# Seven weight blocks prepared on VectorE and kept in DRAM, instead of summed by DMA as they are loaded

## The chip, the cores and the metric

The kernel runs on one core of a Trainium2 chip. The metric is the device time of one execution in microseconds (us). Of the kernel before, three runs were timed: 599.13, 599.25 and 601.3 us, median 599.25. A further execution was profiled; all rows below come from it.

## The reference

Causal attention (2 sequences, 12 heads, 448 positions, 64 columns) is followed by two feed-forward layers on 896 tokens of 768 columns:

```
x = attention(q, k, v)                    # scaled scores, causal mask, softmax, times v
h = x @ w_in;  y = (h * clip(h + 3, 0, 6) / 6) @ w_out              # 768 -> 2048 -> 768
xn = y / sqrt(mean(y*y) + 1e-6) * rms_g
g = xn @ w_gate; val = xn @ w_val
out = (silu(g) * val) @ w_out2                                      # 768 -> 1536 -> 768
```

The weights reach the kernel as the bits of float64, so each block has to be narrowed to float32 on the chip.

## The kernel before

Tokens stand in two groups of 448 columns (g = 0, 1). Every product is taken in three matmuls of 128x128 by 128x448 (`mm3`): weights and data are both split into a high and a low half, and high*high, high*low and low*high are summed. Weights come in blocks of 128x768, numbered 0 to 108 in the order of their use; each holds six 128x128 tiles, so a block serves 18 matmuls, or 36 in `ff2_in`, where both groups use it.

The stages in order: attention, with `ff1_in(0)` beside its end; `ff1_in(1)`; `ff1_out(0)`; `ff1_out(1)` (blocks 48 to 63); `ff2_in` (gate and val, blocks 64 to 87); `strassen` (the last layer, blocks 88 to 108). `strassen` computes the last product by a fast scheme with seven block products of half the size in place of eight: seven products q in the order 1, 5, 6, 7, 3, 4, 2, each with three blocks n = 0 to 2, 378 matmuls in all. Its weight operands are quarters of `w_out2` and sums of them.

The way of a block: `w_load` brings it from DRAM, `w_split` narrows it if it is float64 (two passes on ScalarE, `w_join` on VectorE), `w_halves` writes `whi` on ScalarE, `w_low` writes `wlo` on VectorE and calls `w_load` for the block three later. There are three buffers for `c` (the float32 block) and four each for `whi` and `wlo`.

The operands of the last layer are prepared beside `ff2_in`: `b_prepare` loads one of the twelve float64 blocks into `braw` (a single buffer), `b_narrow` and `b_join` narrow its two sides, and `b_keep` stores them as half blocks of 128x384 into DRAM. Four quarters (named 1, 2, 12, 22) are so kept. Products 1, 3 and 2 load one of them. For products 5, 6, 7 and 4, `w_load` loads a first block and one step later `w_add` adds a second one onto it by a DMA with accumulation, issued from POOL; for 5 and 6 the sum is also stored, since 6 and 4 start from them.

The order on every engine is the order in which the code issues instructions: a clock of steps (nine products' matmuls in each, outside attention), and `at(delay, ...)` puts a piece of work some steps later. All loads and stores named here are issued from one queue, SP, in that order, and an instruction that waits holds up all that stand behind it on its engine.

Of the kernel before, what the change touches and what calls it, by code (L numbers as in the profile page):

```python
# [13 lines left out]
AF = mybir.ActivationFunctionType  # L14
ALU = mybir.AluOpType
# [6 lines left out]
NK = DM // 128  # L22
# [5 lines left out]
NP1 = 16  # L28
NN = NK // 2
ORDER = (1, 5, 6, 7, 3, 4, 2)  # L30
BLOCKS = {1: (1,), 2: (2,), 3: (22,), 5: (12, 1), 6: (5, 22), 7: (12, 22), 4: (2, 6)}
SIDES = {(0, 0): 1, (0, 1): 2, (1, 0): 12, (1, 1): 22}
NEGATED = (1, 22)
NSLOT = 79
MASK = -8e9
NRAW, NC_BUF, NW = 3, 3, 4

# [13 lines left out]
def fused_kernel(ctx: ExitStack, tc, qa, qb, ka, kb, v, w_in, w_out, w_gate, w_val, w_out2, rms_g, out):  # L51
# [5 lines left out]
    nc = tc.nc  # L57

    const = ctx.enter_context(tc.tile_pool(name="const", bufs=1))
    pool = ctx.enter_context(tc.tile_pool(name="pool", bufs=NSLOT))  # L60
    wpool = ctx.enter_context(tc.tile_pool(name="wpool", bufs=1))
# [3 lines left out]
    def psum(name):  # L65
        return pspool.tile([128, 512], F32, tag="ps", name=name)

    def slot(shape, name, dtype=F32):
        return pool.tile(shape, dtype, tag="a", name=name)

    def f32(ap):
        return ap.bitcast(F32)
# [15 lines left out]
    def at(delay, fn, *args):  # L88
        due[clock["now"] + delay].append((fn, args))
# [15 lines left out]
    srcs, kept, parts = [], {}, {}  # L105
# [12 lines left out]
    def w_load():  # L118
        n = state["load"]
        if n >= len(srcs):  # L120
            return
        state["load"] += 1
        if not isinstance(srcs[n], tuple):
            t = wpool.tile([128, 768, 2], U32, tag="raw", name=f"raw{n}", bufs=NRAW)
            nc.sync.dma_start(t.rearrange("p n t -> p (n t)"), srcs[n].bitcast(U32))
            raws[n] = t
            return
        if srcs[n][0] in ("in", "out"):
            found = [kept.pop(srcs[n])]
        else:  # L130
            q, k = srcs[n]
            for p in BLOCKS[q]:
                assert parts[p, k] == 768, (srcs[n], p)
            found = [kept[p, k] for p in BLOCKS[q]]
        c = wpool.tile([128, 768], F32, tag="c", name=f"c{n}", bufs=NC_BUF)
        nc.sync.dma_start(c, found[0])
        plain[n] = c
        if len(found) == 2:
            at(1, w_add, n, c, found[1])

    def w_add(n, c, src):
        nc.gpsimd.dma_start(c, src, accum_op=ALU.add)  # L142
        q, k = srcs[n]
        if q in (5, 6):
            at(2, b_keep, q, k, 0, c)

    def w_split():

# [13 lines left out]
    def narrowed(c, raw, beside):  # L162

        low, high = raw[:, :, 0], raw[:, :, 1]
        byte = raw.rearrange("p n t -> p (n t)").bitcast(U8).rearrange("p (n t) -> p n t", t=8)[:, :, 3]
        if c is not None:
            nc.scalar.activation(c, f32(high), AF.Prelu, scale=2.0 ** -112, alpha=2.0 ** 32)  # L167
        if beside:
            nc.gpsimd.tensor_scalar(low, byte, 1.0 / 32.0, -15.5 / 32.0, op0=ALU.mult, op1=ALU.add)
        else:  # L170
            nc.scalar.activation(low, byte, AF.Copy, scale=1.0 / 32.0, bias=-15.5 / 32.0)  # L171
        return low
# [23 lines left out]
    def w_low(n, c):  # L196
        hi, lo = splits[n]
        nc.vector.tensor_sub(lo, c, f32(hi))  # L198
        if n >= NRAW:
            w_load()  # L200
# [3 lines left out]
    def w_tile(n, j):  # L204

        if n not in used:
            used.add(n)
            splits.pop(n - 2, None)
            at(1, w_split)
        return tuple(t[:, j * 128:(j + 1) * 128] for t in splits[n])  # L210

    def mm3(ps, w, x, first, last, again=False):

        whi, wlo = w
        xhi, xlo = x
        nc.tensor.matmul(ps, whi, xhi, start=first, stop=False, skip_group_check=again)  # L216
        yield
        nc.tensor.matmul(ps, whi, xlo, start=False, stop=False, skip_group_check=again)  # L218
        yield
        nc.tensor.matmul(ps, wlo, xhi, start=False, stop=last, skip_group_check=again)  # L220
        yield
# [6 lines left out]
        at(3, b_narrow, column, part, raw)  # L228

    def b_narrow(column, part, raw):  # L230
        narrowed(None, raw, False)
        pairs = raw[:, :, 1].rearrange("p (k o c) -> p k o c", o=2, c=128)
        for odd in range(2):
            t = f32(pairs[:, :, odd])
            sign = -1.0 if SIDES[column % 2, odd] in NEGATED else 1.0
            nc.scalar.activation(t, t, AF.Prelu, scale=sign * 2.0 ** -112, alpha=2.0 ** 32)
        at(1, b_join, column, part, raw)

    def b_join(column, part, raw):
        pairs = raw.rearrange("p (k o c) t -> p k o c t", o=2, c=128)  # L240
        for odd in range(2):
            t = slot([128, 384], f"b{column}_{part}_{odd}")
            nc.vector.scalar_tensor_tensor(
                t.rearrange("p (k c) -> p k c", c=128).bitcast(U32), pairs[:, :, odd, :, 1], 3, pairs[:, :, odd, :, 0],
                ALU.logical_shift_left, ALU.bitwise_or)
            at(1, b_keep, SIDES[column % 2, odd], column // 2, 384 * part, t)

    def b_keep(p, n, o, t):
        if (p, n) not in kept:
# [155 lines left out]
    def ff1_in(g, w0):  # L405

        for m in range(NF1):
            ps = psum(f"h{g}_{m}")[:, :NT]
            for k in range(NK):
                yield from mm3(ps, w_tile(w0 + m, k), xs[g, k], k == 0, k == NK - 1)  # L410
            at(1, ff1_relu, g, m, ps)
        for k in range(NK):
            xs.pop((g, k))
# [20 lines left out]
    def ff1_out(g, w0):  # L434


        for m in range(NK):
            ps = psum(f"y{g}_{m}")[:, :NT]
            for k in range(NF1):
                i = m * NF1 + k  # L440
                yield from mm3(ps, w_tile(w0 + i // 6, i % 6), gs[g, k], k == 0, k == NF1 - 1)
            at(1, ff1_y, g, m, ps)
        for k in range(NF1):
            gs.pop((g, k))

    left, halves = {"split": set()}, {}
    SOURCE = {1: (0, 0), 2: (0, 1), 4: (1, 1), 7: (1, 0)}

    def sums_first(p):

        t = slot([128, NT], f"s1_{p}")
        nc.vector.tensor_add(t, left[1, 2 * p], left[1, 2 * p + 1])
        left["s1", p] = t
        nc.vector.tensor_sub(left[1, 2 * p], left[1, 2 * p], left[0, 2 * p])
        at(1, sums_second, p)

    def sums_second(p):
        if (1, p) not in left["split"]:
            at(1, sums_second, p)
            return  # L460
        a = left[0, 2 * p]
        nc.vector.tensor_sub(a, a, left["s1", p])
        left["s2", p] = a
        at(1, sums_third, p)

    def sums_third(p):
        t = slot([128, NT], f"s4_{p}")
        nc.vector.tensor_add(t, left[0, 2 * p + 1], left["s2", p])
        left["s4", p] = t

    def a_split(q, p):

        key = {5: ("s1", p), 6: ("s2", p), 3: ("s4", p)}.get(q)
        if key is None:
            g, odd = SOURCE[q]
            key = (g, 2 * p + odd)
        src = left[key]
        hi = slot([128, NT], f"ahi{q}_{p}", F32R)
        lo = slot([128, NT], f"alo{q}_{p}", F32R)
        if q in (1, 3):  # L480
            nc.scalar.mul(hi, src, -1.0)
        else:
            nc.scalar.copy(hi, src)
        halves[q, p] = (hi, lo)
        at(1, a_low, q, p, key, hi, lo, src)

    def a_low(q, p, key, hi, lo, src):
        if q in (1, 3):
            nc.vector.scalar_tensor_tensor(lo, src, -1.0, f32(hi), ALU.mult, ALU.subtract)
        else:  # L490
            nc.vector.tensor_sub(lo, src, f32(hi))
        left["split"].add((q, p))
        if q != 1:
            left.pop(key)
# [146 lines left out]
    def products():  # L641
        yield from ff1_in(0, 0)
        yield from ff1_in(1, NP1)
        yield from ff1_out(0, 2 * NP1)
        yield from ff1_out(1, 3 * NP1)
        for i in range(2 * NK):
            at(6 + 7 * i, b_prepare, i // 2, i % 2)
        yield from ff2_in(IN2)
        yield from strassen(OUT2)

    with tc.manual_schedule():
# [4 lines left out]
        def warm_up(n):  # L656
# [6 lines left out]
        nc.gpsimd.affine_select(  # L663
            out=mask[:, S - C:], in_=mask[:, S - C:], compare_op=ALU.is_ge, fill=MASK,
            base=0, pattern=[[-1, C]], channel_multiplier=1)
# [23 lines left out]
        for n in range(NRAW):  # L689
            plan[12 + 12 * n].append((1, w_load))  # L690
            plan[52 + 6 * n].append((1, w_load))
# [75 lines left out]
```

## Time and profile before

| | us |
|---|---|
| median of three timed runs | 599.25 |
| profiled execution, its own time | 599.7 |
| span of its instructions (first to last) | 597.9 |
| PE busy | 581.3 |
| VectorE (DVE) busy | 363.0 |
| ScalarE (ACT) busy | 357.1 |
| GpSimd (POOL) busy | 97.7 |

PE is the matmul side of TensorE. A matmul of 448 columns is shown as 0.36 to 0.37 us long, but the next one starts 0.20 us after it; so intervals between starts are to be read, not durations. PEclk is the granted clock of TensorE, where 1.00 is full speed.

### The profile page before, as it was taken

How to read it: one execution, taken by the hardware profiler on the slowest of the kernel's cores; microseconds unless marked ns; L12 is line 12 of the kernel's file. 1: busy time of each engine (PE TensorE's matmuls, PEld its weight loads, DVE VectorE, ACT ScalarE, POOL GpSimd, SP SyncE). 2: the span in 40 equal slices, each digit the busy share in tenths (PEclk: the TensorE clock that was granted, in tenths of full speed). 3: DMA queues.
4: the chain of work that ended last, by engine and by line, in shares of the span. 5: the costliest groups of instructions: out<-in, count | busy, mean ns of one | idle time of the engine just before them, and what ended most of it. 6: DMA issues, size and time to landing. Idle time of an engine off the chain costs nothing.

```text
span 597.9 us, 8936 instructions
## 1 busy us (share of the span) xinstructions
PE 581.3 (97%) x3138; PEld 508.4 (85%) x3138; DVE 363.0 (61%) x688; ACT 357.1 (60%) x694; POOL 97.7 (16%) x144
## 2 busy tenths in 40 slices
PE   8889999999999999999999999999999999995997
PEld 6557777778899999999999999999999999984996
DVE  4766767676455576563534576676767664725881
ACT  6998888787455688774325775646365442424450
POOL 4665454543000000010001000000000001111100
PEclk9999999999999999999999999999999999998999
DMA  8968776752233488864254655557565345597761
GB/s 230 275 196 253 230 242 215 213 185 84 77 105 112 184 308 310 322 217 158 85 188 150 212 189 187 200 193 267 177 213 185 133 144 121 158 203 193 204 184 62
DMA packets 41150, 113.06 MB, mean 189 GB/s; under 512 B 5649, under 2 KB 17873, under 8 KB 41105
## 3 DMA queue, kind: packets, MB, share of 16 engines
q1 hardware_dynamic: 38944, 107.42, 54.1%
q0 software_dynamic: 1728, 4.72, 4.8%
q8 instruction: 25, 0.41, 0.3%
q10 hardware_dynamic: 432, 0.34, 0.2%
q14 instruction: 21, 0.16, 0.1%
HBM read 90.05 MB, written 22.41 MB: 188 GB/s over the span
## 4 chain that ended last, share of the span: by engine, by line
PE 85%; ACT 6%; DMA 5%; issue 2%; DVE 1%; SPq 0%; POOLq 0%; ACTq 0%; DVEq 0%
PE f L216 10%; PE f L220 9%; PE f L218 9%; PE y L216 7%; PE y L218 7%; PE y L220 7%; PE h L220 7%; PE h L216 7%; PE h L218 7%; DMA c<-kept 5%; ACT sm L324 4%; PE o L384 3%; PE s L307 3%; PE t L358 3%; ACT pt L368 1%
## 5 line engine op out<-in xcount | busy, mean ns | idle before, releaser
L192 ACT CAST whi<-c 128x768 fp32r<-128x768 f32 x109 | 90.8, 834 | 117.6 <-DVE c L176 57.4
L198 DVE TENSOR_TENSOR wlo<-c,whi 128x768 fp32r<-128x768 f32 x109 | 108.3, 994 | 59.9 <-ACT whi L192 57.6
L216 PE MATMUL f<-yhi,whi 128*128 128x448 f32 x288 | 105.8, 367 | 0.0
L220 PE MATMUL f<-yhi,wlo 128*128 128x448 f32 x288 | 104.9, 364 | 0.0
L218 PE MATMUL f<-ylo,whi 128*128 128x448 f32 x288 | 104.0, 361 | 0.0
L220 PE MATMUL h<-xh,wlo 128*128 128x448 f32 x192 | 72.0, 375 | 0.0
L218 PE MATMUL h<-xl,whi 128*128 128x448 f32 x192 | 70.9, 369 | 0.0
L216 PE MATMUL y<-ghi,whi 128*128 128x448 f32 x192 | 70.5, 367 | 0.0
L216 PE MATMUL h<-xh,whi 128*128 128x448 f32 x192 | 70.4, 367 | 0.0
L220 PE MATMUL y<-ghi,wlo 128*128 128x448 f32 x192 | 70.0, 365 | 0.0
L218 PE MATMUL y<-glo,whi 128*128 128x448 f32 x192 | 69.3, 361 | 0.0
L176 DVE SCALAR_TENSOR_TENSOR c<-c,raw 128x768 uint32<-128x768 uint32 x56 | 55.8, 996 | 20.0 <-ACT raw L171 13.8
L342 POOL TENSOR_SCALAR sm<-sm,st 112x112 f32<-112x112 f32 (+1 forms) x96 | 56.0, 601 | 68.5 <-ACT pt L368 28.8
L220 PEld LDWEIGHTS f<-yhi,wlo 128*128 128x128 f32 x288 | 53.9, 187 | 5.4 <-issue 0.2
L218 PEld LDWEIGHTS f<-ylo,whi 128*128 128x128 f32 x288 | 54.1, 188 | 4.0
L216 PEld LDWEIGHTS f<-yhi,whi 128*128 128x128 f32 x288 | 54.1, 188 | 3.7 <-issue 0.2
L167 ACT ACTIVATE c<-raw 128x768 f32<-128x768 f32 x56 | 50.7, 906 | 3.9 <-DVE wlo L198 3.2
L324 ACT ACTIVATE sm<-sm,st 112x112 f32<-112x112 f32 (+3 forms) x96 | 49.6, 525 | 3.9 <-DVE st L317 3.8
L142 POOL DMA_DIRECT2D c<-kept x12 | 10.4, 865 | 222.0 <-DMA kept<-b 158.6
L220 PEld LDWEIGHTS h<-xh,wlo 128*128 128x128 f32 x192 | 36.0, 188 | 9.3 <-issue 6.7
L421 DVE SCALAR_TENSOR_TENSOR t<-t,h 128x448 f32<-128x448 f32 x32 | 19.8, 620 | 38.7 <-ACT t L417 38.7
L417 ACT ACTIVATE t<-h,half 128x448 f32<-128x448 f32 x32 | 20.5, 639 | 35.4 <-PE h L220 35.4
(109 smaller groups left out, 983.3 us busy)
## 6 DMA issues: line engine op xcount, KB each, us to landing
raw<-in_w_in SPq DMA_DIRECT2D x16, 768.0 KB, 5.3
raw<-in_w_out SPq DMA_DIRECT2D x16, 768.0 KB, 6.1
raw<-in_w_gate SPq DMA_DIRECT2D x12, 768.0 KB, 4.3
raw<-in_w_val SPq DMA_DIRECT2D x12, 768.0 KB, 4.3
braw<-in_w_out SPq DMA_DIRECT2D x12, 768.0 KB, 5.0
c<-kept SPq DMA_DIRECT2D x21, 384.0 KB, 3.7
keptin<-c SPq DMA_DIRECT2D x16, 384.0 KB, 2.7
c<-keptin SPq DMA_DIRECT2D x16, 384.0 KB, 3.0
```

Source lines behind the costliest of these rows:

```text
L167: nc.scalar.activation(c, f32(high), AF.Prelu, scale=2.0 ** -112, alpha=2.0 ** 32)
L176: nc.vector.scalar_tensor_tensor(bits, bits, 3, z, ALU.logical_shift_left, ALU.bitwise_or)
L192: nc.scalar.copy(hi, c)
L198: nc.vector.tensor_sub(lo, c, f32(hi))
L216: nc.tensor.matmul(ps, whi, xhi, start=first, stop=False, skip_group_check=again)
L218: nc.tensor.matmul(ps, whi, xlo, start=False, stop=False, skip_group_check=again)
L220: nc.tensor.matmul(ps, wlo, xhi, start=False, stop=last, skip_group_check=again)
L307: nc.tensor.matmul(ps[:C, o:o + n], tq[64 * j:64 * j + 64, i * C:(i + 1) * C], tk[64 * j:64 * j + 64, 0:n], start=True, stop=True)
L324: nc.scalar.activation(dst, dst, AF.Exp, scale=-1.0, bias=st[u][:, 0, c:c + 1], accum_out=st[u][:, 1, c:c + 1])
L342: nc.gpsimd.tensor_scalar(t[:, o:o + n], t[:, o:o + n], c, 1.0, op0=ALU.mult, op1=ALU.mult)
L417: nc.scalar.activation(t, ps, AF.Relu, bias=half, scale=1.0 / 6.0)
L421: nc.vector.scalar_tensor_tensor(t, t, 1.0, ps, ALU.min, ALU.mult)
```

## The change

All seven weight operands are made beforehand and kept in DRAM, so that the last layer loads one block for each of its 21. `w_add` and the stores of loaded sums are gone. The differences (5: first minus first, 7, 6, 4, named `bt`) are made on VectorE from the narrowed half blocks (`b_sums`, `b_rest`), and all stores go by half blocks. The twelve preparations begin with `ff1_out(1)`, one in six steps, in place of with `ff2_in`, one in seven. `b_narrow` has two full-width passes on ScalarE instead of one full and two half ones. Signs move from the weights to the data: a few subtractions change their order and two `-1` scalings fall away; the number of those instructions stays.

```diff
@@ -28,10 +28,8 @@
 NP1 = 16
 NN = NK // 2
 ORDER = (1, 5, 6, 7, 3, 4, 2)
-BLOCKS = {1: (1,), 2: (2,), 3: (22,), 5: (12, 1), 6: (5, 22), 7: (12, 22), 4: (2, 6)}
-SIDES = {(0, 0): 1, (0, 1): 2, (1, 0): 12, (1, 1): 22}
-NEGATED = (1, 22)
 NSLOT = 79
+PREP, BETWEEN = 4, 6
 MASK = -8e9
...
         if srcs[n][0] in ("in", "out"):
-            found = [kept.pop(srcs[n])]
+            src = kept.pop(srcs[n])
         else:
-            q, k = srcs[n]
-            for p in BLOCKS[q]:
-                assert parts[p, k] == 768, (srcs[n], p)
-            found = [kept[p, k] for p in BLOCKS[q]]
+            src = kept[srcs[n]]
+            assert parts[srcs[n]] == 768, srcs[n]
         c = wpool.tile([128, 768], F32, tag="c", name=f"c{n}", bufs=NC_BUF)
-        nc.sync.dma_start(c, found[0])
+        nc.sync.dma_start(c, src)
         plain[n] = c
-        if len(found) == 2:
-            at(1, w_add, n, c, found[1])
-
-    def w_add(n, c, src):
-        nc.gpsimd.dma_start(c, src, accum_op=ALU.add)
-        q, k = srcs[n]
-        if q in (5, 6):
-            at(2, b_keep, q, k, 0, c)
...
@@ -228,22 +215,41 @@
         at(3, b_narrow, column, part, raw)
 
     def b_narrow(column, part, raw):
-        narrowed(None, raw, False)
-        pairs = raw[:, :, 1].rearrange("p (k o c) -> p k o c", o=2, c=128)
-        for odd in range(2):
-            t = f32(pairs[:, :, odd])
-            sign = -1.0 if SIDES[column % 2, odd] in NEGATED else 1.0
-            nc.scalar.activation(t, t, AF.Prelu, scale=sign * 2.0 ** -112, alpha=2.0 ** 32)
+        c = f32(raw[:, :, 1])
+        narrowed(c, raw, False)
         at(1, b_join, column, part, raw)
+
+    got = {}
 
     def b_join(column, part, raw):
         pairs = raw.rearrange("p (k o c) t -> p k o c t", o=2, c=128)
+        n, j = divmod(column, 2)
         for odd in range(2):
             t = slot([128, 384], f"b{column}_{part}_{odd}")
             nc.vector.scalar_tensor_tensor(
                 t.rearrange("p (k c) -> p k c", c=128).bitcast(U32), pairs[:, :, odd, :, 1], 3, pairs[:, :, odd, :, 0],
                 ALU.logical_shift_left, ALU.bitwise_or)
-            at(1, b_keep, SIDES[column % 2, odd], column // 2, 384 * part, t)
+            got[odd, j] = t
+            if (odd, j) != (0, 1):
+                at(1, b_keep, {(0, 0): 1, (1, 0): 2, (1, 1): 3}[odd, j], n, 384 * part, t)
+        if j == 1:
+            at(1, b_sums, n, part)
+
+    def b_sums(n, part):
+        b_minus(5, n, part, got[0, 1], got[0, 0])
+        b_minus(7, n, part, got[1, 1], got[0, 1])
+        at(1, b_rest, n, part)
+
+    def b_rest(n, part):
+        b_minus(6, n, part, got[1, 1], got["t", 5])
+        b_minus(4, n, part, got[1, 0], got["t", 6])
+        got.clear()
+
+    def b_minus(p, n, part, a, b):
+        t = slot([128, 384], f"bt{p}_{n}_{part}")
+        nc.vector.tensor_sub(t, a, b)
+        got["t", p] = t
+        at(1, b_keep, p, n, 384 * part, t)
 
     def b_keep(p, n, o, t):
         if (p, n) not in kept:
...
-        nc.vector.tensor_sub(left[1, 2 * p], left[1, 2 * p], left[0, 2 * p])
+        nc.vector.tensor_sub(left[1, 2 * p], left[0, 2 * p], left[1, 2 * p])
         at(1, sums_second, p)
 
...
         a = left[0, 2 * p]
-        nc.vector.tensor_sub(a, a, left["s1", p])
+        nc.vector.tensor_sub(a, left["s1", p], a)
         left["s2", p] = a
         at(1, sums_third, p)
 
     def sums_third(p):
         t = slot([128, NT], f"s4_{p}")
-        nc.vector.tensor_add(t, left[0, 2 * p + 1], left["s2", p])
+        nc.vector.tensor_sub(t, left[0, 2 * p + 1], left["s2", p])
         left["s4", p] = t
 
     def a_split(q, p):
...
         lo = slot([128, NT], f"alo{q}_{p}", F32R)
-        if q in (1, 3):
-            nc.scalar.mul(hi, src, -1.0)
-        else:
-            nc.scalar.copy(hi, src)
+        nc.scalar.copy(hi, src)
         halves[q, p] = (hi, lo)
         at(1, a_low, q, p, key, hi, lo, src)
 
     def a_low(q, p, key, hi, lo, src):
-        if q in (1, 3):
-            nc.vector.scalar_tensor_tensor(lo, src, -1.0, f32(hi), ALU.mult, ALU.subtract)
-        else:
-            nc.vector.tensor_sub(lo, src, f32(hi))
+        nc.vector.tensor_sub(lo, src, f32(hi))
         left["split"].add((q, p))
         if q != 1:
             left.pop(key)
...
@@ -642,9 +642,10 @@
         yield from ff1_in(0, 0)
         yield from ff1_in(1, NP1)
         yield from ff1_out(0, 2 * NP1)
+        for i in range(2 * NK):
+            n, rest = divmod(i, 4)
+            at(PREP + BETWEEN * i, b_prepare, 2 * n + rest % 2, rest // 2)
         yield from ff1_out(1, 3 * NP1)
-        for i in range(2 * NK):
-            at(6 + 7 * i, b_prepare, i // 2, i % 2)
         yield from ff2_in(IN2)
         yield from strassen(OUT2)
 

```

PE's order is the same in both kernels. Three places where others differ:

SP and POOL in the last layer, before: `c91` to `c93` are the blocks of product 5, `c94` to `c96` of product 6, `c97` on of product 7; `kept12_0` is quarter 12 of block column 0. SP:

```order
L136 DMA c92_5103<-kept12_1_4503 128x768
L254 DMA kept5_1_5139<-c92_5103 128x768
L136 DMA c93_5156<-kept12_2_4945 128x768
L254 DMA kept5_2_5193<-c93_5156 128x768
L136 DMA c94_5220<-kept5_0_5083 128x768
L136 DMA c95_5260<-kept5_1_5139 128x768
L254 DMA kept6_0_5276<-c94_5220 128x768
L136 DMA c96_5297<-kept5_2_5193 128x768
L254 DMA kept6_1_5313<-c95_5260 128x768
L136 DMA c97_5338<-kept12_0_4062 128x768
L254 DMA kept6_2_5352<-c96_5297 128x768
```

Between the loads stand stores of sums, which wait for the accumulating loads. Those stand on POOL, in the same stage:

```order
L142 DMA c91_5044<-kept1_0_3839 128x768
L142 DMA c92_5103<-kept1_1_4281 128x768
L142 DMA c93_5156<-kept1_2_4721 128x768
L142 DMA c94_5220<-kept22_0_4064 128x768
L142 DMA c95_5260<-kept22_1_4505 128x768
L142 DMA c96_5297<-kept22_2_4947 128x768
L142 DMA c97_5338<-kept22_0_4064 128x768
L142 DMA c98_5374<-kept22_1_4505 128x768
L142 DMA c99_5405<-kept22_2_4947 128x768
```

Each adds a second quarter onto a block that SP has loaded. SP at the same place now:

```order
L132 DMA c91_5109<-kept5_0_3468 128x768
L132 DMA c92_5163<-kept5_1_3884 128x768
L132 DMA c93_5213<-kept5_2_4291 128x768
L132 DMA c94_5274<-kept6_0_3489 128x768
L132 DMA c95_5313<-kept6_1_3908 128x768
L132 DMA c96_5347<-kept6_2_4312 128x768
L132 DMA c97_5385<-kept7_0_3470 128x768
L132 DMA c98_5418<-kept7_1_3886 128x768
L132 DMA c99_5448<-kept7_2_4293 128x768
```

Nine loads stand one behind the other; the stores between them are gone, and POOL issues nothing any more in this stage.

VectorE in `ff1_out(1)` before, around blocks 54 to 58 (`ylo` belongs to the layer's result):

```order
L198 TENSOR_TENSOR wlo54_3337<-c54_3266,whi54_3336 128x768
L198 TENSOR_TENSOR wlo55_3361<-c55_3293,whi55_3360 128x768
L567 SCALAR_TENSOR_TENSOR ylo1_1_3392<-y1_1_3299,gvec_74,yhi1_1_3376 128x448
L198 TENSOR_TENSOR wlo56_3390<-c56_3323,whi56_3389 128x768
L198 TENSOR_TENSOR wlo57_3417<-c57_3349,whi57_3416 128x768
L198 TENSOR_TENSOR wlo58_3441<-c58_3374,whi58_3440 128x768
```

Here it has only the low halves of blocks and of the result. The same place now (`b` are narrowed half blocks, `bt` the differences):

```order
L229 SCALAR_TENSOR_TENSOR b0_0_0_3340<-braw0_0_3277 128x384
L229 SCALAR_TENSOR_TENSOR b0_0_1_3342<-braw0_0_3277 128x384
L185 TENSOR_TENSOR wlo54_3345<-c54_3266,whi54_3344 128x768
L185 TENSOR_TENSOR wlo55_3375<-c55_3295,whi55_3374 128x768
L567 SCALAR_TENSOR_TENSOR ylo1_1_3406<-y1_1_3301,gvec_74,yhi1_1_3390 128x448
L185 TENSOR_TENSOR wlo56_3404<-c56_3327,whi56_3403 128x768
L229 SCALAR_TENSOR_TENSOR b1_0_0_3432<-braw1_0_3372 128x384
L229 SCALAR_TENSOR_TENSOR b1_0_1_3434<-braw1_0_3372 128x384
L250 TENSOR_TENSOR bt5_0_0_3450<-b1_0_0_3432,b0_0_0_3340 128x384
L250 TENSOR_TENSOR bt7_0_0_3452<-b1_0_1_3434,b1_0_0_3432 128x384
L185 TENSOR_TENSOR wlo57_3437<-c57_3361,whi57_3436 128x768
L250 TENSOR_TENSOR bt6_0_0_3472<-b1_0_1_3434,bt5_0_0_3450 128x384
```

Four joins and four differences of 128x384 now stand between the `wlo` of blocks that PE is about to use.

SP in `ff1_out(1)` before, around blocks 56 to 60:

```order
L136 DMA c56_3323<-keptout_8_2913 128x768
L136 DMA c57_3349<-keptout_9_2943 128x768
L136 DMA c58_3374<-keptout_10_2973 128x768
L136 DMA c59_3405<-keptout_11_3011 128x768
L136 DMA c60_3429<-keptout_12_3041 128x768
```

It has loads of blocks alone. The same place now:

```order
L132 DMA c56_3327<-keptout_8_2913 128x768
L260 DMA kept1_0_3356<-b0_0_0_3340 128x384
L260 DMA kept2_0_3358<-b0_0_1_3342 128x384
L132 DMA c57_3361<-keptout_9_2943 128x768
L214 DMA braw1_0_3372<-in_w_out2 128x1536
L132 DMA c58_3388<-keptout_10_2973 128x768
L132 DMA c59_3421<-keptout_11_3011 128x768
L260 DMA kept3_0_3448<-b1_0_1_3434 128x384
L132 DMA c60_3455<-keptout_12_3041 128x768
L214 DMA braw0_1_3466<-in_w_out2 128x1536
L260 DMA kept5_0_3468<-bt5_0_0_3450 128x384
L260 DMA kept7_0_3470<-bt7_0_0_3452 128x384
```

Loads of `braw` and stores of half blocks, which wait for VectorE, now stand between the loads of blocks.

## Rows read from the trace of the kernel before

**Rows 1.** The page: span; busy time by engine.

```profile
span 597.9 us, 8936 instructions
PE 581.3 (97%) x3138; PEld 508.4 (85%) x3138; DVE 363.0 (61%) x688; ACT 357.1 (60%) x694; POOL 97.7 (16%) x144
...
```

**Rows 2.** Busy time by stretch; columns named in the first row.

```profile
core 0: us, PE busy (x) PEld busy (x) DVE busy (x) ACT busy (x) POOL busy (x), PEclk, DMA share, GB/s
215.80:274.10 58.30, 58.30 (x290) 54.05 (x289) 34.75 (x39) 40.81 (x55) 4.65 (x4) 1.00 0.80 282
274.10:333.00 58.90, 58.90 (x291) 54.29 (x290) 26.58 (x27) 25.84 (x36) 5.81 (x5) 1.00 0.43 142
333.00:508.46 175.46, 175.46 (x867) 162.34 (x867) 112.59 (x168) 96.68 (x140) 3.05 (x3) 1.00 0.55 184
508.46:537.62 29.16, 29.16 (x146) 26.84 (x144) 14.70 (x23) 10.41 (x19) 4.23 (x5) 1.00 0.73 181
537.62:554.70 17.08, 10.64 (x41) 8.57 (x41) 9.77 (x16) 9.15 (x16) 1.69 (x2) 0.80 0.74 187
```

**Rows 3.** Timeline of PE: first and last matmul of the last layer, three stops.

```profile
508.50 0.37 PE L216 MATMUL w<-ahi,whi 128*128 128x448 f32 x1
...
538.43 0.47 PE L216 MATMUL y<-ahi,whi 128*128 128x448 f32 x1 [0.64 <-ACT whi L192]
...
549.98 0.74 PE L216 MATMUL y<-ahi,whi 128*128 128x448 f32 x1 [4.63 <-ACT ahi L483]
551.57 0.74 PE L218 MATMUL y<-alo,whi 128*128 128x448 f32 x1 [0.85 <-DVE alo L491]
...
593.92 0.36 PE L220 MATMUL x<-ahi,wlo 128*128 128x448 f32 x1
```

**Rows 4.** Timeline of ACT behind the longest stop.

```profile
548.63 0.83 ACT L192 CAST whi<-c 128x768 fp32r<-128x768 f32 x1 [7.32 <-DMA c<-kept]
549.37 1.03 ACT L483 CAST ahi<-u 128x448 fp32r<-128x448 f32 x2
```

**Rows 5.** Part of the chain of waits: start us, us, what.

```profile
532.54 4.90 DMA c<-kept
537.46 0.32 SPq L254
...
537.88 4.25 DMA c<-kept
...
542.66 5.89 DMA c<-kept
```

**Rows 6.** What the SP queue waited for, 500 to 560 us.

```profile
SPq L254 <- DMA c<-kept: 30.7, 5, 8.0
```

**Rows 7.** DMA issues of the page: count, KB each, us to landing.

```profile
braw<-in_w_out SPq DMA_DIRECT2D x12, 768.0 KB, 5.0
c<-kept SPq DMA_DIRECT2D x21, 384.0 KB, 3.7
...
c<-kept POOLq DMA_DIRECT2D x12, 384.0 KB, 5.4
...
```

**Rows 8.** DMA issues, 215.8 to 274.1 us alone.

```profile
raw<-in_w_out SPq DMA_DIRECT2D x11, 768.0 KB, 6.4
...
```

**Rows 9.** Instructions by line and shape, 274.1 to 508.5 us.

```profile
L198 DVE TENSOR_TENSOR wlo<-c,whi 128x768 fp32r<-128x768 f32 x41 | 40.9, 999 | 20.3 <-ACT whi L192 20.1
L192 ACT CAST whi<-c 128x768 fp32r<-128x768 f32 x40 | 33.4, 834 | 54.0 <-DVE c L176 37.6 <-PE y L218 14.9 <-PE f L218 1.5
...
L167 ACT ACTIVATE c<-raw 128x768 f32<-128x768 f32 x24 | 21.4, 891 | 3.2 <-DVE wlo L198 3.2
...
L243 DVE SCALAR_TENSOR_TENSOR b<-braw 128x384 uint32<-128x384 uint32 x24 | 12.2, 551 | 0.0
...
L171 ACT ACTIVATE braw<-braw 128x768 uint32<-128x768 uint8 x12 | 10.7, 895 | 0.8 <-DMA braw<-in_w_out 0.8
```

**Rows 10.** Timeline of ACT in the second output layer.

```profile
289.35 0.84 ACT L192 CAST whi<-c 128x768 fp32r<-128x768 f32 x1 [2.80 <-PE y L218]
```

More of the change, by code (lines that the diff above doesn't have):

```diff
@@ L165, in narrowed @@
         byte = raw.rearrange("p n t -> p (n t)").bitcast(U8).rearrange("p (n t) -> p n t", t=8)[:, :, 3]
-        if c is not None:
-            nc.scalar.activation(c, f32(high), AF.Prelu, scale=2.0 ** -112, alpha=2.0 ** 32)
+        nc.scalar.activation(c, f32(high), AF.Prelu, scale=2.0 ** -112, alpha=2.0 ** 32)
         if beside:
```

## The prediction

> **What bounds the kernel now.** I read the page first: PE is busy for 581.3 of 597.9 us [rows 1]; so only time in which PE stops, or work that leaves PE, can move the end, and PE's list of matmuls stays as it is. Next the stretches [rows 2]: from 215.8 to 508.46 us PE is busy without a gap at full clock (before that lies attention, which the change doesn't touch); in 537.62 to 554.70 us it starts 41 matmuls in 17.08 us and its granted clock falls to 0.80. That is inside the last layer, the only place after 216 us where PE stands still. Then the timeline of PE there [rows 3]: a stop of 0.64 us that ends with a `whi`, one of 4.63 us that ends with an `ahi` on ACT, one of 0.85 us that ends with the `alo` behind it. The reader might blame the data halves `ahi`; ACT's own timeline says otherwise [rows 4]: the `ahi` that PE waited for is behind a `whi` for which ACT had been idle for 7.32 us, until a block from DRAM had landed. The chain of waits says why the block was late [rows 5]: accumulating load (4.90 us), SP's issue of the store of the sum, which waited for it, the next plain load (4.25), the next accumulating load (5.89). SP spent 30.7 us in this stage in front of such stores [rows 6], with the next blocks' loads queued behind. A block thus needs a plain load and an accumulating one in series, 3.7 and 5.4 us in the median [rows 7], and part of this does not overlap between blocks, while PE uses up a block in 18 matmuls.
>
> **What the stops cost.** From 333.00 to 508.46 us PE runs 866 matmuls (867 are shown, one reaches in from before) in 175.46 us [rows 2], one in 0.2026 us. The last layer has 7 x 3 x 6 x 3 = 378, which need 378 x 0.2026 = 76.6 us. It takes from 508.50 to 593.92 plus 0.20, 85.6 us [rows 3]. So 9.0 us are lost, the slow clock after the long stop included.
>
> **The change, part by part.**
>
> *Removed: twelve accumulating loads, six stores of loaded sums.* With one load per block, `w_low` of a block issues the load for the block three later, and PE takes 3 x 18 x 0.2026 = 10.9 us for three blocks. A plain load lands in 3.7 us [rows 7], then come `whi` (0.83) and `wlo` (1.0) [rows 9]: 5.5 of 10.9 us. `ff1_out(1)` runs just so, with the same sizes and the same 18 matmuls per block, and PE has no gap there in 58.90 us [rows 2]. I take the whole 9.0 us back. From both sides: it cannot be more, since PE would then run without a gap to the end; the least that this removal alone gives is nothing, if the blocks were late for another reason (a rival below). Nearest row: `ff1_out(1)`, hence the whole.
>
> *Added on VectorE: 24 differences of 128x384.* The trace has no subtraction of this size. A join of 128x384 takes 0.551 us and a two-operand pass over 128x768 0.999 [rows 9]; I take 0.55, the row with the same size, so 24 x 0.55 = 13.2 us (bounds: nothing and 24.0). None of it is on PE's path while VectorE has room: in `ff1_out(1)` it is busy for 26.6 of 58.9 us [rows 2], and five preparations (ten joins, eight differences) bring 18 x 0.55 = 9.9 us; in `ff2_in` 112.6 of 175.5 us are busy, and ten joins less and sixteen differences more make 3.3 us. Cost 0.
>
> *Moved: twelve preparations, from `ff2_in` into `ff1_out(1)` and the front of `ff2_in`.* Five of them (steps 4, 10, 16, 22 and 28 of the 32 of that layer) fall where a block lasts 3.65 us and not 7.3. What matters is how far ahead of PE the blocks are there. ACT's `whi` at 289.35 us began when PE left a block, after 2.80 us of idling [rows 10]: it is not short of data but of one of four buffers, so it writes for the block three later, 10.9 us ahead of its use. Of these `whi` and `wlo` take 1.8, and 9.1 are spare. A preparation puts two passes on ACT between them, 0.89 each [rows 9], 1.8 us, and on VectorE up to two joins and four differences, 3.3 us: 4.0 us stay. Cost 0. If the cover were gone, each would cost PE up to 5.1 us.
>
> *Queues.* SP carries 42 stores of half blocks in place of 24 and 6; those of `b` and `bt` now wait for VectorE with the loads of blocks 57 to 63 and of `raw` and `braw` behind them. Each stands in the order behind work that is due a step before it, and the load behind it waits for a `wlo` that VectorE does later still; so I count no hold. The bytes: `ff1_out(1)` has 142 GB/s, 8.4 MB in 58.9 us [rows 2]; five loads of 0.79 MB and 14 stores of 0.20 MB make 15.0 MB, 255 GB/s. The stretch before it ran at 282 GB/s with PE never stopped [rows 2]. Cost 0.
>
> *Load on the transfers.* At 282 GB/s a load of 768 KB landed in 6.4 us [rows 8], while `braw`, of the same size, takes 5.0 in its quieter stretch [rows 7]: 1.4 us more, which the 4.0 us that stay cover. The Trainium skill speaks against the change here (DMA: Bandwidth & Descriptors, Latency and other measured facts): HBM access takes 0.2 us on average and up to 2 at high load, so moving transfers into a stretch with others makes all of them slower; by that rule it would be 1.8 us for each (an estimate from the page), with the sum unchanged, and the slower rival below would set in 1.8 us earlier. The rows agree in direction.
>
> *Signs.* As many instructions as before, of the same shapes. Nothing.
>
> **The sum.** 599.7 (the profiled execution's own time) - 9.0 + 0 = 590.7 us. That execution is 0.45 us above the median of 599.25, so on the scale of the median 590.25; I put 590.4, leaving a little for a first block that comes late.
>
> **Rivals.**
>
> 1. *Part of the stop stays.* For it: all transfers of the last layer still share SP's queue with the stores of the result, and 0.73 to 0.74 of the DMA time was in use there [rows 2]. Against: the accumulating loads and the stores of sums go, and plain loads alone never held PE [rows 2, 10]. If half of the loss stays: 599.7 - 4.5 = 595.2.
> 2. *The data halves are the limit.* PE's longest stop ended with `ahi` [rows 3]; if ACT or VectorE were late with these on their own, single loads would not help. For it only that row; against it ACT's idle time of 7.32 us right in front [rows 4]. Time: 599.25 as before.
> 3. *Slower: ACT stands behind `braw` in `ff1_out(1)`.* ACT takes its work in order. If a `braw` (one buffer, loaded only after the join before it, behind SP's waiting stores) lands late, ACT stops and with it every `whi` behind. It decides from 4.0 us of lateness; to eat the whole gain, five preparations have to be 4.0 + 9.0 / 5 = 5.8 us late each, and for 0.5% above the old time (3.0 us more) 6.4. At 8 us: 5 x 4.0 = 20, so 599.7 - 9.0 + 20 = 610.7. For it: SP has waits of up to 8.0 us [rows 6]. Against: ACT waited for `braw` only 0.8 us in all twelve preparations [rows 9], which are as far behind their loads in steps (three) as now.
>
> **Chances and range.** Forecast 0.82, rival 1 0.11, rival 2 0.04, rival 3 0.03. The forecast alone: 589.3 (0.9 below, for runs that differ) to 591.8. The range takes in the near half of rival 1: 589.3 to 593.8. A measurement of this kernel tells about 0.5% from no change, 3.0 us: faster means under 596.25. Forecast and most of rival 1 are there, 0.92; within 0.5% are rival 2 and the rest of rival 1, 0.05; slower is rival 3, 0.03.
>
> **What the new profile would show.** If right: span about 588.9; the last layer takes 76.6 us with PEclk 1.00 throughout; no accumulating load, no wait of SP in front of a store for a load; ACT's `whi` there ends its idle time on PE, not on `c<-kept`; 24 differences near 0.55 us; PE without a gap from 274 us on. Wrong would be: an idle time of PE in `ff1_out(1)` or early `ff2_in` that ends with `whi` or `wlo` (rival 3, with ACT idle on `braw`), or one in the last layer that ends with `ahi` while ACT had the block in time (rival 2).

## The result, and the profile after

The changed kernel takes 590.41 us in the median of four runs (589.90 to 590.92); the kernel before, now with a fourth run beside it, 599.97. The ratio is 0.9839, with a 95% interval of 0.9814 to 0.9863. The profiled execution took 589.9 us over a span of 588.1. Of one kernel below (plain loads with six stores) one run in four took 1145 us, with no trace of it, and its median is given without it.

The page after: span, busy time by engine, PE's busy tenths and its granted clock in 40 slices.

```profile
span 588.1 us, 8933 instructions
PE 578.7 (98%) x3138; PEld 507.6 (86%) x3138; DVE 375.2 (64%) x712; ACT 356.5 (61%) x682; POOL 87.2 (15%) x132
...
PE   8899999999999999999999999999999999999997
...
PEclk9999999999999999999999999999999999999999
...
```

The stretch of before in which PE was busy for 10.64 of 17.08 us, at a clock of 0.80 [rows 2], is gone: neither PE's tenths nor its clock fall there. Of the busy times only VectorE's has grown, by 12.2 us [rows 1]; POOL has lost its 10.5 us of accumulating loads.

The stretches after, for `ff1_out(1)`, `ff2_in` and the last layer:

```profile
core 0: us, PE busy (x) PEld busy (x) DVE busy (x) ACT busy (x) POOL busy (x), PEclk, DMA share, GB/s
...
273.70:332.60 58.90, 58.90 (x291) 54.29 (x290) 34.41 (x43) 33.60 (x46) 5.82 (x5) 1.00 0.73 254
332.60:508.04 175.44, 175.44 (x867) 162.31 (x866) 116.18 (x174) 88.20 (x119) 1.17 (x1) 1.00 0.48 162
508.04:584.70 76.66, 76.65 (x380) 70.70 (x378) 49.43 (x77) 32.23 (x55) 0.00 (x0) 1.00 0.34 111
...
```

PE is busy throughout in all three, at full clock. `ff1_out(1)` now moves 254 GB/s in place of 142 and has VectorE busy for 34.4 us in place of 26.6 [rows 2]. The last layer takes up the window of 76.66 us.

First and last matmul of the last layer on PE's timeline:

```profile
508.08 0.37 PE L203 MATMUL w<-ahi,whi 128*128 128x448 f32 x1
...
584.32 0.37 PE L207 MATMUL x<-ahi,wlo 128*128 128x448 f32 x1
```

From start to start this is 76.24 us; before it was 593.92 - 508.50 = 85.42 [rows 3]. The difference, 9.18 us, is nearly the whole of the span's 9.8. Of the rest, 0.42 us lie in front of the last layer (508.50 to 508.08; the first matmul of `ff1_in` is already 0.43 us earlier, in a part that the change leaves alone), and 0.20 behind its last matmul.

ACT's timeline in the middle of the last layer; the bracket is its idle time and what ended it:

```profile
529.92 0.84 ACT L179 CAST whi<-c 128x768 fp32r<-128x768 f32 x1 [1.87 <-PE z L205]
530.66 1.03 ACT L486 CAST ahi<-u 128x448 fp32r<-128x448 f32 x2
...
```

Before, ACT waited here for a block from DRAM, up to 7.32 us [rows 4]. Now its `whi` waits until PE leaves a buffer, as in `ff1_out(1)` [rows 10]: the blocks are early.

The longest wait of the SP queue, 500 to 560 us:

```profile
SPq L132 <- DVE wlo L185: 47.5, 15, 7.1
...
```

No store of a sum stands in front of a load any more [rows 6]; SP waits for `wlo`, that is for a free buffer of `c`. Stores of the result still stand there, and SP waits 7.8 us in front of them, but PE has no gap.

The new and moved work by line and shape, 273.7 to 508 us (count, busy time and mean ns, idle time in front):

```profile
L229 DVE SCALAR_TENSOR_TENSOR b<-braw 128x384 uint32<-128x384 uint32 x24 | 12.3, 554 | 6.6 <-ACT braw L158 6.6
...
L154 ACT ACTIVATE braw<-braw 128x768 f32<-128x768 f32 x12 | 10.9, 906 | 10.1 <-DMA braw<-in_w_out 10.1
...
L250 DVE TENSOR_TENSOR bt<-b,bt 128x384 f32<-128x384 f32 x12 | 6.7, 555 | 0.3
L250 DVE TENSOR_TENSOR bt<-b,b 128x384 f32<-128x384 f32 x12 | 6.1, 552 | 0.0
```

A difference of 128x384 takes 552 to 555 ns. But ACT now waits 10.1 us in all for `braw`, before only 0.8 [rows 9]. Part of the reason stands in the DMA issues (count, KB each, median us to landing):

```profile
braw<-in_w_out SPq DMA_DIRECT2D x12, 768.0 KB, 5.7
...
c<-kept SPq DMA_DIRECT2D x21, 384.0 KB, 3.0
...
kept<-bt SPq DMA_DIRECT2D x24, 192.0 KB, 5.3
kept<-b SPq DMA_DIRECT2D x18, 192.0 KB, 2.5
```

A `braw` lands after 5.7 us in place of 5.0 [rows 7], a plain block of the last layer after 3.0 in place of 3.7. The longest of ACT's waits has a second reason: SP issues the load late. SP's timeline there, then ACT's:

```profile
355.10 0.79 SPq L260 DMA_DIRECT2D kept<-b  x2
355.98 0.45 SPq L214 DMA_DIRECT2D braw<-in_w_out  x1
...
```

```profile
362.57 0.91 ACT L154 ACTIVATE braw<-braw 128x768 f32<-128x768 f32 x1 [3.57 <-DMA braw<-in_w_out]
...
```

ACT was ready for this `braw` at 359.00, only 3.0 us after its load was issued; the code leaves three steps between them, 5.5 us of PE's time. Right in front of it SP stood until VectorE had written the `b` to be stored.

### The profile page after: what moved, and what is told of

Its sections match the earlier page's. It is cut to its first block, busy times and chain, and to the rows that moved or that the text cites. A ratio compares the mean times of both kernels' runs of the same rounds, so it can differ in the third digit from the quotient of the medians.

```text
span 588.1 us, 8933 instructions
## 1 busy us (share of the span) xinstructions
PE 578.7 (98%) x3138; PEld 507.6 (86%) x3138; DVE 375.2 (64%) x712; ACT 356.5 (61%) x682; POOL 87.2 (15%) x132
## 4 chain that ended last, share of the span: by engine, by line
PE 93%; ACT 6%; issue 1%; DVE 0%; DVEq 0%
PE f L203 10%; PE f L207 10%; PE f L205 10%; PE y L203 8%; PE y L207 8%; PE y L205 8%; PE h L207 7%; PE h L203 7%; PE h L205 7%; ACT sm L330 4%; PE o L390 3%; PE t L364 3%; PE s L313 3%; PE z L203 1%; PE z L207 1%; PE z L205 1%
## 5 line engine op out<-in xcount | busy, mean ns | idle before, releaser
L323 DVE CUSTOM_DVE_ANT_0 sm<-s,mask 112x112 f32<-112x112 f32 (+3 forms) x96 | 37.3, 443 | 5.9 <-PE s L313 5.6
```

The source lines that it names most:

```text
L323: nc.vector.tensor_tensor_reduce(dst, src, mask[:, S - n:], scale=-0.125, scalar=3e38, op0=ALU.add, op1=ALU.min, accum_out=st[u][:, 0, c:c ...
```

## Experiments

Each was timed beside the kernel before on the same chip (medians 599.2 to 600.5), and its ratio is to those runs; the first two rows are those of the result. The last layer is given from its first to its last matmul's start.

| kernel | median us | ratio to before (95%) | last layer us |
|---|---|---|---|
| before | 599.97 | | 85.42 |
| changed | 590.41 | 0.984 (0.981 to 0.986) | 76.24 |
| changed, late preparations | 590.54 | 0.986 (0.983 to 0.988) | 76.24 |
| before, early preparations | 599.02 | 1.000 (0.998 to 1.002) | 85.14 |
| before, no stores of sums | 591.50 | 0.988 (0.985 to 0.990) | 76.33 |
| changed, six stores added | 589.99 | 0.985 (0.981 to 0.988) | 76.24 |
| before, stores later | 594.99 | 0.992 (0.990 to 0.995) | 81.30 |
| before, stores later, fourth c | 590.72 | 0.985 (0.982 to 0.988) | 76.24 |
| before, fourth c | 592.69 | 0.988 (0.986 to 0.991) | 77.86 |
| changed, one preparation in 4 steps | 596.35 | 0.994 (0.991 to 0.997) | 76.24 |
| changed, differences 4 times | 614.94 | 1.024 (1.019 to 1.029) | 76.24 |
| changed, differences twice | 590.19 | 0.985 (0.981 to 0.989) | 76.24 |

**The two halves of the change apart.** The late preparations in the changed kernel:

```diff
-        for i in range(2 * NK):
-            n, rest = divmod(i, 4)
-            at(PREP + BETWEEN * i, b_prepare, 2 * n + rest % 2, rest // 2)
         yield from ff1_out(1, 3 * NP1)
+        for i in range(2 * NK):
+            n, rest = divmod(i, 4)
+            at(6 + 7 * i, b_prepare, 2 * n + rest % 2, rest // 2)
```

Expected: 

> The changed kernel, with the twelve preparations put back beside ff2_in (one in seven steps from its sixth step on). Theory A (the gain is the single plain load for each block of the last layer; when the blocks are prepared does not matter): PE again without a gap in the last layer, 76.2 us from its first to its last matmul, median within 0.3% of the changed kernel's 590.4 us. Rival C (the earlier preparation brought part of it, because the last layer's first loads wait for stores that come late): a stop of some us at the start of the last layer, 593 us or more.

First and last matmul of the last layer on PE's timeline:

```profile
508.58 0.37 PE L203 MATMUL w<-ahi,whi 128*128 128x448 f32 x1
...
584.82 0.37 PE L207 MATMUL x<-ahi,wlo 128*128 128x448 f32 x1
```

76.24 us, as in the changed kernel to 0.01 us. The other half, early preparations in the kernel before:

```diff
+        for i in range(2 * NK):
+            at(4 + 6 * i, b_prepare, i // 2, i % 2)
         yield from ff1_out(1, 3 * NP1)
-        for i in range(2 * NK):
-            at(6 + 7 * i, b_prepare, i // 2, i % 2)
```

Expected: 

> The kernel before, with its twelve preparations moved into ff1_out(1), one in six steps, and the sums still made by accumulating loads. Theory A: the stop stays, about 9 us lost in the last layer, median about 600 us. Rival C (the earlier preparation brought the gain): at most half of it is left, 595 us or less.

PE's timeline at the stops:

```profile
539.13 0.47 PE L216 MATMUL y<-ahi,whi 128*128 128x448 f32 x1 [1.64 <-ACT whi L192]
...
549.42 0.47 PE L216 MATMUL y<-ahi,whi 128*128 128x448 f32 x1 [1.80 <-ACT ahi L483]
551.01 0.74 PE L218 MATMUL y<-alo,whi 128*128 128x448 f32 x1 [1.12 <-DVE alo L491]
...
```

The stops are there again, the first longer and the second shorter than before [rows 3], 0.28 us less in all. So the whole gain comes from how the blocks are loaded, and none from when they are prepared. (The passes of `b_narrow` and the signs were not put back alone; a kernel below that has the old ones reaches 76.24 us too.)

**Accumulation or stores.** Six stores taken out of the kernel before:

```diff
-BLOCKS = {1: (1,), 2: (2,), 3: (22,), 5: (12, 1), 6: (5, 22), 7: (12, 22), 4: (2, 6)}
+BLOCKS = {1: (1,), 2: (2,), 3: (22,), 5: (12, 1), 6: (12, 22), 7: (12, 22), 4: (2, 22)}
...
         nc.gpsimd.dma_start(c, src, accum_op=ALU.add)
-        q, k = srcs[n]
-        if q in (5, 6):
-            at(2, b_keep, q, k, 0, c)
```

Expected: 

> The kernel before without the six stores of loaded sums; products 6 and 4 take quarters 12 + 22 and 2 + 22 in place of the stored sums, so their operands are other numbers; all twelve accumulating loads stay. Theory A in its narrow form (the stores in front of which SP waits for the accumulation put the blocks in series; without them plain load 3.7, accumulating load 5.4, whi and wlo 1.8 us take 10.9 of the 10.9 us that a block has): at most 1.5 us lost in the last layer, median 590 to 592.5 us. Rival B (the accumulating loads alone are too slow): at least 5 us still lost, 596 us or more.

Products 6 and 4 are here loaded from other quarters, as many and as large, so that no stored sum is needed; the kernel computes another result, and no load has to wait for a stored sum either. ACT's timeline in the middle of the last layer:

```profile
530.40 0.83 ACT L189 CAST whi<-c 128x768 fp32r<-128x768 f32 x1 [3.27 <-DMA c<-kept]
...
539.15 0.83 ACT L189 CAST whi<-c 128x768 fp32r<-128x768 f32 x1 [2.19 <-DMA c<-kept]
...
544.37 0.83 ACT L189 CAST whi<-c 128x768 fp32r<-128x768 f32 x1 [3.45 <-PE y L217]
...
```

ACT waits for blocks until 539 us, so these are later than in the changed kernel, but PE loses only 0.09 us. All twelve accumulating loads are there: they alone are not too slow. The counterpart, plain loads with six stores behind them:

```diff
             src = kept[srcs[n]]
+            if srcs[n][0] in (5, 6):
+                at(3, w_again, n)
...
+    def w_again(n):
+        q, k = srcs[n]
+        t = dram.tile([128, 768], F32, name=f"again{q}_{k}")
+        nc.sync.dma_start(t, held_c.pop(n))
```

Expected: 

> The changed kernel with six stores added where the kernel before had them: each loaded block of products 5 and 6 is stored once more to DRAM, from SP, behind its load. Theory A (such a store costs PE only as long as SP waits in front of it, now about 3 us of a plain load instead of 9 us of two, less than the 3.65 us in which PE uses a block): no loss, 590.4 us within 0.3%. Rival D (any store that SP waits for between the loads is enough to bring the stop back): 3 us or more lost in the last layer, 593.5 us or more.

What the SP queue waited for, 500 to 560 us:

```profile
SPq L134 <- DVE wlo L196: 38.1, 15, 4.2
...
SPq L142 <- DMA c<-kept: 5.1, 2, 2.6
...
```

SP now waits at most 2.6 us in front of such a store (8.0 before [rows 6]), and PE loses nothing. With three buffers the stop needs both, accumulating loads and stores that wait for them.

**Stores later, and a miss.** The stores stay, further back on SP:

```diff
-            at(2, b_keep, q, k, 0, c)
+            at(6 if (q, k) in ((5, 0), (5, 1)) else 4, b_keep, q, k, 0, c)
```

Expected: 

> The kernel before with its accumulating loads and all six stores of sums; only their place on SP is later, so that in product 6 the load three blocks on (before: two) and in product 5 the load two blocks on (before: the next) is the first one behind a store. Theory A in its narrow form (plain load, accumulating load and SP's wait in front of the store, about 9.6 us, are paid once for as many blocks as the store stands back): 4.8 us a block in product 5, which is loaded while PE takes 7.3 us a block, and some 4.3 us, with the store's own landing, in product 6 against PE's 3.65, less than the 7 us that are spare; at most 2 us lost in the last layer, 590.5 to 592.5 us. Rival (the stores or the bytes themselves cost it, wherever they stand): 596 us or more.

Less than half came back, 4.1 of 9.2 us. The chain of waits (start, us, what):

```profile
523.78 6.26 DMA c<-kept
530.14 0.84 ACT whi L192
...
531.99 0.32 SPq L136
532.40 6.49 DMA kept<-c
...
538.96 4.34 DMA c<-kept
...
543.84 5.94 DMA c<-kept
...
```

SP's wait in front of the stores is nearly gone (3.3 us in place of 30.7 [rows 6], 500 to 560 us). In its place stands the store's own landing: the load three blocks on goes into the buffer that the store reads, and here it waits for a store that takes 6.49 us. In the median these six stores took 4.0 us, in the kernel before 2.9. To tell this apart, a fourth buffer (and one slot less, for room) was added, once to this kernel and once to the kernel before:

```diff
-NSLOT = 79
+NSLOT = 78
-NRAW, NC_BUF, NW = 3, 3, 4
+NRAW, NC_BUF, NW = 3, 4, 4
```

Expected with the later stores: 

> The kernel before with the later stores of sums, which had still lost 5.1 us in the last layer, and a fourth buffer for c (one of the 79 slots is given up for it). Theory E (what was left came from the buffers: the load three blocks on goes into the buffer that the late store still reads, and a store takes up to 6.5 us to land): at most 2 us lost in the last layer, 590.5 to 592.5 us. Rival B again (accumulating loads and stores together are too much for the transfers, wherever they stand): 594 us or more, as with three buffers.

Expected for the kernel before: 

> The kernel before with the fourth buffer for c alone (78 slots). Theory A (SP's wait in front of the stores puts the blocks in series, and a buffer more does not change what SP has behind them): 7 us or more still lost in the last layer, 597 to 600 us. If the buffers alone were the limit: 593 us or less.

With later stores the fourth buffer brings the rest: 76.24 us, no loss. But in the kernel before the buffer alone leaves 1.6 us of loss where I had written 7 or more: a miss. SP's waits there, 500 to 560 us:

```profile
SPq L254 <- DMA c<-kept: 32.1, 5, 7.9
```

They are as long as before [rows 6]. What differs is the start. First and last accumulating loads for products 5 to 7 on POOL's timeline, with the fourth buffer:

```profile
490.06 1.02 POOL L142 DMA_DIRECT2D c<-kept  x1 [153.99 <-DVE b L243]
...
537.12 1.81 POOL L142 DMA_DIRECT2D c<-kept  x2 [6.24 <-DVE u L531]
...
```

and in the kernel before:

```profile
494.23 1.02 POOL L142 DMA_DIRECT2D c<-kept  x1 [158.63 <-DMA kept<-b]
...
521.69 0.85 POOL L142 DMA_DIRECT2D c<-kept  x1 [7.78 <-DVE alo L491]
...
544.75 0.84 POOL L142 DMA_DIRECT2D c<-kept  x1 [1.23 <-DMA c<-kept]
...
```

With four buffers the series begins 4.2 us earlier, since the first load finds a free buffer earlier (read from the order of events, not tried apart), and the ninth block (the second of the two at 537.12) is some 6.7 us ahead. Without the buffer the six loads onto `c94` to `c99` start 4.6 us apart in the mean (521.69 to 544.75), while PE uses up a block in 3.65. With it they are still slower than PE (4.2), but the lead lasts nearly to their end: PE stops once, for 1.12 us. So the narrow form of my theory, that SP's waits alone make the stop, falls.

**How near the edge the moved work is.** The changed kernel with `BETWEEN = 4` in place of 6.

Expected: 

> The changed kernel with a preparation in four steps in place of six. The mechanism of the slower rival (ACT behind a braw that is late) should now decide: load 5.7, two passes 1.8, joins 1.1 us and the issue make about 9 us for each preparation, while four steps of ff1_out(1) last 7.3; over the eight preparations of that stage 14 us of lateness gather, against 6 to 9 us that are spare: 4 to 8 us of PE idle in ff1_out(1) that end with whi, 594.5 to 598.5 us. If the cover is larger than I think: 590.4 us within 0.3%, with ACT waiting longer for braw than the 10.1 us of the changed kernel.

ACT's timeline at the end of `ff1_out(1)`, then PE's:

```profile
329.69 0.91 ACT L154 ACTIVATE braw<-braw 128x768 f32<-128x768 f32 x1 [5.85 <-DMA braw<-in_w_out]
...
331.26 0.90 ACT L154 ACTIVATE c<-raw 128x768 f32<-128x768 f32 x1
...
333.98 0.83 ACT L179 CAST whi<-c 128x768 fp32r<-128x768 f32 x1
...
```

```profile
334.86 0.47 PE L203 MATMUL f<-yhi,whi 128*128 128x448 f32 x1 [1.30 <-ACT whi L179]
...
338.06 0.74 PE L207 MATMUL f<-yhi,wlo 128*128 128x448 f32 x1 [2.52 <-DVE wlo L185]
...
```

The slower rival's mechanism exists: ACT stands for 5.85 us in front of a `braw`, the block behind it is narrowed too late, and PE stops at the start of `ff2_in`. The median of 596.35 is 2.9 us under the kernel before beside it (599.23), with runs from 592.35 to 598.16; the forecast of 594.5 to 598.5 holds for the time, but not for the place. That is a little further on than I had put it: PE lost nothing within `ff1_out(1)`, but at the first float64 block behind it, which needs two more passes on ACT and one on VectorE.

The differences four times, then twice:

```diff
-        nc.vector.tensor_sub(t, a, b)
+        for _ in range(4):
+            nc.vector.tensor_sub(t, a, b)
```

Expected: 

> The changed kernel with each of the 24 differences computed four times (72 more subtractions of 128x384, the same result). Theory (VectorE's work is off PE's path as long as it fits what is spare in front of PE): 12 more of 0.55 us, 6.6 us, in each pair of steps, against the 6.4 us that were least spare in ff1_out(1): 0 to 1.5 us slower, 590.4 to 592 us. Rival (each microsecond of VectorE's added work shows): 72 x 0.55 = 39.6 us more, over 600 us.

A miss by 23 us. VectorE's timeline in front of PE's longest stop, and the stop:

```profile
382.68 1.03 DVE L229 SCALAR_TENSOR_TENSOR b<-braw 128x384 uint32<-128x384 uint32 x2 [3.79 <-ACT braw L158]
...
385.15 4.58 DVE L251 TENSOR_TENSOR bt<-b,b 128x384 f32<-128x384 f32 x8
...
391.38 4.71 DVE L251 TENSOR_TENSOR bt<-b,bt 128x384 f32<-128x384 f32 x8
396.00 0.95 DVE L185 TENSOR_TENSOR wlo<-c,whi 128x768 fp32r<-128x768 f32 x1
...
```

```profile
397.01 0.74 PE L207 MATMUL f<-yhi,wlo 128*128 128x448 f32 x1 [5.81 <-DVE wlo L185]
```

VectorE waits 3.79 us for a narrowed half, then sixteen subtractions take 9.3 us of the next 11, and `wlo` comes behind them. PE stops for 2.85, 3.47 and 3.84 us more at 335.96, 424.20 and 451.71. I had taken the least spare time of `ff1_out(1)`, where PE lost nothing; what broke is `ff2_in`, from its front on. With each difference twice:

Expected: 

> The changed kernel with each of the 24 differences computed twice, after four times of each took 614.9 us. Theory (it was not each added microsecond that showed, but VectorE's room in the front of ff2_in: there the changed kernel has it busy for up to 18.2 of 21.9 us, the time of two preparations; three more of each of four differences, 6.6 us, go over it, one more, 2.2 us, makes 20.4 and fits): at most 1 us slower than the changed kernel, 590 to 591.5 us. Rival (added work shows in proportion, as 24.5 us for 72 subtractions suggest): 24 x 0.34 = 8 us, 598 us.

A stretch of 21.9 us, two preparations long, with the busiest VectorE (columns as above):

```profile
343.00:364.90 21.90, 21.90 (x110) 20.31 (x109) 20.34 (x30) 14.16 (x18) 0.00 (x0) 1.00 0.57 193
...
```

In the changed kernel VectorE is busy for 18.57 us of the same stretch. Full to 20.34, as expected, and no loss, 590.19 us. So the cost is not in proportion: up to twice the work is free, four times is not. No version here beats the changed kernel by more than these runs tell apart, and none can by feeding PE better: from 273.7 us to the end of the last layer PE has no idle time left.

## Why the prediction was right, point by point

**What the stops cost.** Predicted 9.0 us, measured 9.18 from first to last matmul. Taking PE's own interval from the undisturbed stage as the yardstick was enough; the slow clock after the stop was contained in it and went with it. The idle times alone would have priced it too low: the three stops of [rows 3] come to 6.12 us.

**The removal gives all of it back.** Right: 76.24 us, and ACT waits for PE, not for blocks. The late preparations with plain loads give the same, and early ones with sums by DMA give 0.28 us.

**Why the blocks were late.** Half right. The prediction named SP's wait in front of the stores, with loads queued behind. Without the stores only 0.09 us are lost, which agrees. But the fourth buffer recovers 7.6 of 9.2 us with SP's waits as long as ever. What the runs show is a supply of blocks slower than PE's use (4.6 us a block against 3.65 in products 6 and 7), made of a plain load, an accumulating load, a wait on SP and three buffers; easing any one of three links (stores, buffers, accumulation) is enough or nearly so, though stores that are only placed later give back less than half. How each microsecond is shared between them was not measured.

**24 differences at 0.55 us, hidden.** The size is right (0.552 and 0.555). Hidden is right, but the argument was thin: the prediction compared busy time over the whole of `ff2_in`, 115.9 of 175.5 us, and it measures 116.18. The load is not even:

```profile
...
354.50:376.40 21.90, 21.90 (x110) 20.31 (x109) 18.21 (x31) 14.05 (x20) 0.00 (x0) 1.00 0.75 260
...
442.10:464.00 21.90, 21.90 (x110) 20.29 (x109) 13.06 (x19) 9.13 (x13) 0.00 (x0) 1.00 0.37 126
...
```

In the front of the stage VectorE is busy for 18.2 of 21.9 us (18.6 in the fullest stretch of that length), in its second half for 13.1. These rows of the changed kernel, not the mean, say how much more would fit, and four times the differences showed it.

**The preparations beside `ff1_out(1)`.** Cost 0 is right. The least lead of a `wlo` there was put at 4.0 us; the tightest block (56) has 6.8: its `wlo` ends at 297.1 us, and PE first uses it at 303.9. In the kernel before this block had 7.0; the most that any block lost is 2.2 (57, from 9.5 to 7.3), where the prediction took 5.1. Predicted bytes 255 GB/s, measured 254. Mis-sized was ACT's wait for `braw`: counted as none, it is 10.1 us over twelve, 1.7 of them in `ff1_out(1)`, all under cover.

**Queues.** "No hold" is wrong, though it cost nothing: in `ff1_out(1)` SP stood 11.1 us in front of stores that waited for `b` (five times, 6.2 us at most), and 29.4 us between 332.6 and 420. Being due a step after the join did not mean that VectorE had done it by then.

**Load on the transfers.** The prediction allowed 1.4 us more for a `braw` in `ff1_out(1)`. The five loads there landed after 5.0 us in the median, no later than before; the seven behind them took 6.1, and the loads for gate rose from 4.3 to 5.4. The Trainium skill (DMA: Bandwidth & Descriptors, Latency and other measured facts) has HBM access at 0.2 us on average and up to 2 at high load. These two rises lie under the 1.8 us that the prediction estimated from it; that of the stores of 192 KB does not (1.9 us before, 5.3 for those of `bt`). No run shows what part of them is HBM access. The sum did not change, since PE waited for none of these transfers.

**Rivals.** The first (half of the stop stays) and the second (the data halves) did not come; `ahi` was only queued behind `whi`. The third has its mechanism shown at four steps, and its time at the distance chosen here is zero.

**The time.** 590.4 against 590.41. The closeness is partly luck: the kernel before came out at 599.97 with the fourth run, not 599.25, and two of the changed kernel's runs lie at 589.9 and two at 590.9.

## What to carry to other kernels

Before replacing a summing load, look at what is queued behind it: here a store that waited for the sum held back the next loads, and one more buffer alone would have recovered 7.6 of the 9.2 us, with later stores all of it. Judge whether added work hides by the fullest stretch of the engine that takes it, as long as one period of that work, and by what it waits for itself, not by the mean over a stage. To price a stop, use the unhindered interval of the same instructions elsewhere in the trace: it gave 9.0 of 9.18 us.

## What the runs showed of the hardware that had not been expected

A store of 192 KB landed after 1.9 us in the median in the kernel before, where two follow each other. The 24 stores of `bt` took 5.3; the eight of them in `ff1_out(1)`, four within some 2.3 us right behind a load of `braw`, took 6.4. The 18 single or paired ones of `b` took 2.5. The six stores of 384 KB took 2.9 us in the kernel before and 4.0 where they were issued later, the longest 6.49. What makes them land later was not tried.
